# Decay differences of two chunks as two products a batch from sums spread over heads, and chunk 0's mixing placed behind its factors

## The chip, the core and the metric

The kernel runs on one core of a Trainium2 chip. Its engines run side by side, each through its own list of instructions in order: TensorE (PE: matrix products; PEld: the weight loads that go with them), VectorE (DVE), ScalarE (ACT), GpSimd (POOL), and SyncE (SP), which issues most DMA transfers. Products land in PSUM, in eight banks; everything else lies in SBUF, 128 partitions wide. The metric is the device time of one launch in microseconds.

## What is computed

A Mamba-2 state-space layer is followed by a feed-forward block with hardswish. Batch 4, 8 heads, 768 positions, head size 32, state size 16; the feed-forward has 256 inputs and 2048 hidden units. The reference, cut to what matters:

```python
log_a = np.log(np.clip(a, 1e-06, 1.0))
for c in range(nc):
    cum = np.cumsum(la, axis=-1)
    L = np.exp(cum[:, :, :, None] - cum[:, :, None, :]) * causal
    M = np.einsum('bhin,bhjn->bhij', Cc, Bc) * L
    y[:, :, sl] = np.einsum('bhij,bhjd->bhid', M, xc) + inter
    state = decay_full[:, :, None, None] * state + np.sum(Bx, axis=2)
...
h = x @ w_in
g = h * np.clip(h + 3.0, 0.0, 6.0) / 6.0
return g @ w_out
```

`x` of the last part is `y` with the heads laid side by side, 3072 rows of 256.

## The kernel before

The sequence is cut into 6 chunks of 128 positions, each handled as two halves of 64. For each chunk there is an attention part (decays, scores, mixing, state) and a feed-forward part (hidden layer, output layer). The program is one list written out by hand; each engine gets its instructions in that order, and tiles bring waits by themselves. The part of chunk 0 comes first; then the loop over `k` runs the feed-forward of chunk `k` and weaves the attention of chunk `k + 1` into it.

**Decays of chunks 0 and 1.** The running sum of log a (`cum`, L282) has 32 rows, one for each pair of batch and head. `in_three` (L286) splits the sums of the first 256 positions into three bf16 parts, 96 rows of `split`. For a batch, a PSUM bank `d` of 128 x 8 x 64 first takes the causal mask (L352). `diff_less` (L364) subtracts each position's own sum with one product of 512 columns. `diff_pick` (L373) adds the sum at the later position: `pick` has one column for each batch and head, with ones in that pair's three rows, so each head and half takes a product of its own, 64 columns wide, 16 a batch. `diff_exp` (L381) takes the exponential on ScalarE. `ends` (L412, GpSimd) scales B with the last column of the decays.

**Scores and mixing of chunk 0.** `turn_squares` (L481) transposes C on VectorE, `part_heads` (L488) parts its heads. `scores` runs the products L543 and those that go into the state (L555). `multiply` takes the sums out of PSUM on ScalarE (L571, L580) and multiplies the decays with the scores on VectorE (L585, four). `mix` has two parts `u`, four heads each: products L611 and then, for chunk 0, L516 from the middle state. `keep` copies the four quarters of y out of PSUM (L625, ScalarE) into `yT`. `renew` makes chunk 1's incoming state (L594, two L565 on VectorE). `turn_cum` transposes the later running sums on TensorE (L329), `by_token` negates them (L332). `busy` is a product with no use for the result (L506, one fp32 product in two passes).

**Weights.** They come as float64 in four quarters of `w_in` and four of `w_out`, 1 MB each, on the DMA queues, and `decode(i)` makes fp32 of them in five steps, one for each call of `weights(i, 1)`:

- step 1: L206 on ScalarE (copies the top 16 bits out); for quarter 0 also L209 and L213 on VectorE
- step 2: L223 and L225 on VectorE, which read what L206 wrote; then L209 for the others
- step 3: L229 on ScalarE
- step 4: L231 on ScalarE; L213 for the others; the load three quarters ahead (L143, SP)
- step 5: L236 and L249 on VectorE; L249 gives the finished weights

**Chunk 0's feed-forward.** `mlp_in` (L636) multiplies `yT` with the quarters of `w_in`, 16 blocks `f` of 512 columns in four rotating banks f0 to f3; ScalarE's L715 and VectorE's L720 make the hardswish of each, and steps of `decode` are woven between them. Then `first_out` (L735) multiplies with `w_out`. In that stretch VectorE also makes the split weights of the later chunks (L658, L663), the faded C of chunk 1 (L463) and its decays times scores (L585); L675 and L678 split its y, and the first product of the next hidden layer (L684) uses that.

**Banks.** Chunk 0's four `d` lie in f0 to f3, those of chunk 1 in the output banks (batches 0 and 1) and in y0 and y1 (batches 2 and 3). The scores take f0 to f3 again, the second halves of y take f0 and f1, `c_ps` of `turn_cum` takes f1, the bank of `busy` f0.

Of the kernel before, what the change touches and what calls it, by code (L numbers as in the profile page):

```python
# [21 lines left out]
def kernel(  # L22
# [172 lines left out]
    def decode(i):  # L195

        n = NK * FP * P  # L200
        top = raws[i].bitcast(U16).rearrange("p (n w) -> p n w", w=4)[:, :, 3]
        lo, hi = (raws[i].rearrange("p (n w) -> p n w", w=2)[:, :, w] for w in range(2))
        se = att.tile([P, 2, n], U16, name="wse")
        s, e = se[:, 0], se[:, 1]
        m = att.tile([P, n], U32, name="wm")
        nc.scalar.copy(out=s, in_=top)  # L206

        def significand():
            nc.vector.tensor_scalar(  # L209
                out=m, in0=hi, scalar1=0xFFFFF, scalar2=0x100000,  # L210
                op0=ALU.bitwise_and, op1=ALU.bitwise_or)
            yield
            nc.vector.scalar_tensor_tensor(  # L213
                out=m.bitcast(FP32), in0=lo, scalar=2.0 ** -32, in1=m, op0=ALU.mult,
                op1=ALU.add)
            yield

        parts_m = significand()
        if i == 0:
            next(parts_m)  # L220
            next(parts_m)
        yield
        nc.vector.tensor_scalar(  # L223
            out=e, in0=s, scalar1=0x7FF0, scalar2=None, op0=ALU.bitwise_and)
        nc.vector.tensor_scalar(  # L225
            out=s, in0=s, scalar1=0x8000, scalar2=None, op0=ALU.bitwise_and)
        next(parts_m, None)
        yield
        nc.scalar.activation(e.bitcast(BF16), e, AF.Relu, bias=bias_hi, scale=-8.0)  # L229
        yield  # L230
        nc.scalar.activation(e, e.bitcast(BF16), AF.Relu, bias=bias_lo, scale=-1.0)  # L231
        next(parts_m, None)
        if i and i + NRAW < 2 * NP:
            load_w(i + NRAW)
        yield
        nc.vector.tensor_tensor(out=e, in0=e, in1=s, op=ALU.bitwise_or)  # L236
        m, e = m.bitcast(FP32), e.bitcast(BF16)
        if i < NP:
            if i < 2:
                dst = att.tile([P, NK, FP * P], FP32, name="w32", tag="y", bufs=3)  # L240
            else:
                dst = ffn.tile([P, NK, FP * P], FP32, name="w32", tag=("wide", "back")[i - 2])
            first_in[i] = dst
            m, e = (t.rearrange("p (k f) -> p k f", k=NK) for t in (m, e))
        else:
            dst = w_out[:, (i - NP) * FP:(i - NP + 1) * FP, :]
            m, e = (t.rearrange("p (k f) -> p k f", k=FP) for t in (m, e))
        unit = 2.0 ** -20 if i >= NP else 2.0 ** -20 / Z
        nc.vector.scalar_tensor_tensor(  # L249
            out=dst, in0=m, scalar=unit, in1=e, op0=ALU.mult, op1=ALU.mult)  # L250
# [6 lines left out]
    picks = ffn.tile([P, G * N], BF16, name="picks", tag="u2")  # L257
    mid = pre[:G, 9].bitcast(BF16)[:, :2 * P]
    low = pre[:G, 10, :2 * P]

    cum = pre[:G, 4:6].rearrange("g t i -> g (t i)")[:, :S]
    cum_c = cum.rearrange("g (c p) -> g c p", p=P)
# [2 lines left out]
    def row_signs():  # L265
        with nc.allow_low_precision("zeros and ones"):
            nc.vector.tensor_reduce(
                out=pick, in_=ident[:, :pad].rearrange("g (r q) -> g q r", r=3), axis=AX.X,
                op=ALU.add)
        nc.scalar.mul(less, pick, -1.0)  # L270
        nc.gpsimd.tensor_copy(
            picks.rearrange("k (g n) -> k g n", n=N), pick.unsqueeze(2).to_broadcast([P, G, N]))
        nc.vector.tensor_reduce(
            out=parity, in_=head.rearrange("p q t -> p t q"), axis=AX.X, op=ALU.add)
# [11 lines left out]
    def in_three():  # L286
        first = cum[:, :2 * P]
        part = split.rearrange("g c p -> g (c p)")
        nc.vector.tensor_copy(part[:G], first)
        nc.vector.tensor_tensor(out=low, in0=first, in1=part[:G], op=ALU.subtract)  # L290
        nc.vector.tensor_copy(mid, low)
        nc.vector.tensor_copy(part[G:2 * G], mid)
        nc.vector.tensor_tensor(out=part[2 * G:pad], in0=low, in1=mid, op=ALU.subtract)
# [42 lines left out]
    def y_tile(name, dtype):  # L336
        return att.tile([P, NK, TB], dtype, name=name, tag="y", bufs=3)
# [28 lines left out]
            rhs=less[:, b * NH:(b + 1) * NH].unsqueeze(2).to_broadcast([P, NH, HT]),  # L366
            start=False, stop=True, skip_group_check=True)

    def diff_pick(c, b):
        for h in range(NH):  # L370
            for a, rows in enumerate(HALF):
                g = b * NH + h
                nc.tensor.matmul(  # L373
                    out=ds[c, b][rows, h], lhsT=pick[:, g:g + 1].to_broadcast([P, HT]),
                    rhs=split[:, c, rows], start=False, stop=True,
                    tile_position=(0, a * HT), skip_group_check=True)

    def diff_exp(c, b):
        if c not in Ls:
# [63 lines left out]
    def turn_b(c):  # L443

        t_ps = turn_ps(c, 1)
        transposes(c, 1, t_ps)
        nc.scalar.copy(out=turned(c)[0], in_=t_ps)
# [169 lines left out]
        if c and 1 in parts:  # L617
            from_state(c, 1)

    def keep(c):  # L620

        yTs[c] = y_tile("yT", FP32)
        for u in range(2):
            for a in range(2):
                nc.scalar.copy(out=y_half(yTs[c], a, u), in_=ys[c][a, u])  # L625

    def y_half(t, a, u):
        return t[:, u].rearrange("p (b i) -> p b i", b=NB)[:, :, HALF[a]]
# [330 lines left out]
    def weights(i, n):  # L959
        for _ in range(n):  # L960
            next(parts[i], None)


    def diff(c, *bs):
        for part in (diff_less, diff_pick):
            for b in bs:
                part(c, b)

    for c in range(2):
        for b in range(NB):  # L970
            diff_mask(c, b)
# [2 lines left out]
    row_signs()  # L974
    add_up(ends_at[0])
    in_three()
    for b in range(2):
        mask_again(0, b)
    diff(0, 0, 1)
    diff(0, 2, 3)  # L980
    weights(0, 1)
    for b in range(NB):
        diff_exp(0, b)
    first_eto()
    diff(1, 2, 3)
    weights(0, 1)
    for b in range(NB):
        ends(0, b)
    turn_b(0)
    diff(1, 0, 1)  # L990
    busy(1, ps.tile([P, NB * P], FP32, name="d", tag="f0"))
    weights(0, 1)
    diff_exp(1, 2)
    diff_exp(1, 3)
    turn_squares(bcs[0][0], turned(0)[2])
    part_heads(0)
    fade(0, HALF[1], nc.gpsimd)
# [4 lines left out]
    scores(0)  # L1002
    multiply(0)
    load_w(3)
    c_ps = ps.tile([P, NC, G], FP32, name="c_ps", tag="f1")
    turn_cum(c_ps)
    busy(1, ps.tile([P, NB * P], FP32, name="d", tag="f0"))
    weights(0, 1)
    weights(1, 1)
    by_token(c_ps)  # L1010
    mix(0)
    keep(0)
    weights(1, 3)
    renew(0)
    weights(1, 1)
    load_eto(1)
    load_bc(1)
    load_x(1)
# [7 lines left out]
    for k in range(NC):  # L1026
        gTs[k] = ffn.tile([P, NF, TB], FP32, name="gT")
        c, ahead = k + 1, k + 2
        if k == 0:
            for f in range(NF):  # L1030
                mlp_in(k, f)
                for i in weave.get(f, []):
                    weights(i, 1)
                if f in (6, 8):
                    diff_exp(c, f // 2 - 3)
            load_bc(ahead)
            weights(NP + 1, 1)
            weights(NP + 3, 1)
            weights(NP + 2, 3)
            sums = weight_sums()  # L1040
            for i in range(NP):
                for b in range(NB):
                    first_out(b, i, c)
                    if (i, b) == (0, 0):
                        weights(NP + 3, 1)
                        weights(NP + 2, 1)
                        weights(NP + 3, 3)
                        rows(ahead)
                    elif (i, b) == (1, 0):
                        for j in range(NP - 1):  # L1050
                            high_w(j)
                        for j in range(2):
                            low_w(j)
                            gap_w(j)
                    elif (i, b) == (2, 0):
                        turn(c, 1)
                        wake(c)
                        turn(c, 0)
                        low_w(2)
                        gap_w(2)  # L1060
                        high_w(NP - 1)
                        for p in range(2):
                            conceal(ahead, p)
                    elif (i, b) == (2, 3):
                        scores(c)
                        multiply(c)
                        renew(c)
                        decay_ends(ahead, 0)
                        decay_ends(ahead, 1)
                        next(sums)  # L1070
                    elif (i, b) == (3, 1):
                        results(c)
                        next(sums)
                        next(sums)
                        decay_ends(ahead, 2)
                        load_x(ahead)
            rows(ahead + 1)
            continue
# [89 lines left out]
```

## Time and profile before

| | us |
|---|---|
| median of 3 runs (lowest, highest) | 345.66 (345.23, 345.81) |
| the profiled execution's own time | 345.45 |
| its span, first to last instruction | 343.7 |
| TensorE busy, VectorE busy, ScalarE busy, GpSimd busy | 334.6, 220.1, 173.2, 142.7 |
| first L543 (scores of chunk 0) | 14.86 |
| first L636 (chunk 0's hidden layer) | 22.98 |
| first L735 (chunk 0's output layer) | 50.55 |
| first L684 (chunk 1's hidden layer) | 82.85 |

The granted clock is full in all 40 slices. A line of the timeline has start, duration, engine, source line, operation, tiles written and read, shapes, how many, and in brackets the idle time of the engine before it and what ended it. "issue" there means that no semaphore which the profile shows ended it. A row of a stage table has the stretch, its length, and for each engine the busy time and how many instructions. One L506, L543, L611 or L636 of the source is two passes on TensorE, and the profile counts passes. The queue q8 of the DMA view carries instructions.

### The profile page before, as it was taken

The numbers are of one execution on the slowest core, as the hardware profiler recorded it, in microseconds if no ns is written. First come the engines' busy times: TensorE is split into PE (matmuls) and PEld (weight loads), VectorE is DVE, ScalarE is ACT, GpSimd is POOL, SyncE is SP. The second block draws the span as 40 slices with busy tenths as digits, with TensorE's granted clock in tenths as the row PEclk, the third lists the DMA queues.
The fourth block names the chain that finished last, engine by engine and source line by source line (L and its number), as shares of the span: only waits on it lengthen the run. The fifth ranks groups of instructions, "written<-read, shape, count | busy, mean of one in ns | idle before, by whom it ended". The sixth has DMA issues, their size and how long they took to land.

```text
span 343.7 us, 8181 instructions
## 1 busy us (share of the span) xinstructions
PE 334.6 (97%) x3378; PEld 266.5 (78%) x3378; DVE 220.1 (64%) x357; ACT 173.2 (50%) x359; POOL 142.7 (42%) x139
## 2 busy tenths in 40 slices
PE   6889999999999999999999999999999999999996
PEld 2554448888778888888888888888887788888995
DVE  6689999999698647775438666447666324676011
ACT  4769878738874561564551564561564010565000
POOL 3300000093299923099611199610099400089500
PEclk9999999999999999999999999999999999999999
DMA  8888959206941057242029242051200010200010
GB/s 173 163 341 169 242 187 176 53 2 95 192 61 23 5 69 159 34 60 51 2 34 176 46 56 58 6 64 17 34 13 0 2 19 1 34 12 2 0 33 31
DMA packets 91605, 24.89 MB, mean 72 GB/s; under 512 B 84208, under 2 KB 87952, under 8 KB 91056
## 3 DMA queue, kind: packets, MB, share of 16 engines
q1 hardware_dynamic: 87184, 23.06, 34.8%
q10 hardware_dynamic: 4384, 1.31, 1.7%
q8 instruction: 26, 0.43, 0.5%
q14 instruction: 11, 0.09, 0.1%
HBM read 21.07 MB, written 3.29 MB: 71 GB/s over the span
## 4 chain that ended last, share of the span: by engine, by line
PE 75%; issue 11%; DMA 4%; DVE 2%; ACT 2%; POOL 2%; SPq 2%; POOLq 0%; DVEq 0%
PE h L684 31%; PE wb L861 13%; PE wc L861 8%; PE wa L861 8%; PE oa L794 4%; PE ob L794 4%; PE y L611 2%; PE y L516 2%; DMA raw<-in_moe_w_in_dram 2%; PE cb L543 2%; DMA eto<-cum_e 1%; ACT L L401 1%; POOL bs L412 1%; DMA pairs<-in_C_dram 1%; SPq L321 1%
## 5 line engine op out<-in xcount | busy, mean ns | idle before, releaser
L708 DVE SCALAR_TENSOR_TENSOR gT<-gT,h 128x512 f32<-128x512 f32 x80 | 54.9, 687 | 30.7 <-ACT gT L707 27.9
L707 ACT ACTIVATE gT<-h,half_up 128x512 f32<-128x512 f32 x80 | 55.1, 690 | 33.2 <-PE h L684 33.1
L780 POOL TENSOR_TENSOR s<-gT 128x512 f32<-128x512 f32 x20 | 25.8, 1288 | 66.4 <-DVE gT L708 66.4
L684 PE MATMUL h<-gap,w_gap 128*128 128x512 f32 x160 | 51.8, 409 | 0.0
L684 PE MATMUL h<-high,w_high 128*128 128x512 f32 x160 | 50.7, 398 | 0.1
L684 PE MATMUL h<-low,w_low 128*128 128x512 f32 x160 | 50.3, 395 | 0.0
L700 ACT ACTIVATE h<-h 128x512 f32<-128x512 f32 x40 | 23.5, 588 | 30.4 <-PE h L684 30.4
L684 PEld LDWEIGHTS h<-high,w_high 128*128 128x128 f32 x160 | 29.5, 188 | 8.5 <-DVE h L697 2.1
L684 PEld LDWEIGHTS h<-low,w_low 128*128 128x128 f32 x160 | 30.1, 188 | 7.2
L684 PEld LDWEIGHTS h<-gap,w_gap 128*128 128x128 f32 x160 | 29.9, 188 | 7.1 <-DVE gap L678 0.5
L401 ACT ACTIVATE L<-L,cum_n 128x64 f32<-128x64 f32 x128 | 31.6, 337 | 0.7 <-POOL L L162 0.7
L861 PE MATMUL wb<-s,w_out 128*128 128x256 f32 x128 | 30.7, 382 | 0.0
L419 POOL TENSOR_TENSOR tmp<-state,eto 128x256 f32<-128x256 f32 x5 | 3.6, 721 | 61.0 <-ACT eto L405 60.9
L735 PE MATMUL o<-w_out,gT 128*128 128x256 f32 x128 | 28.7, 381 | 0.0
L697 DVE TENSOR_SCALAR h<-h 128x512 f32<-128x512 f32 x40 | 27.7, 692 | 1.2 <-PE h L684 1.2
L636 PE MATMUL h<-yT,w 128*128 128x512 f32 x64 | 27.7, 594 | 0.0
L780 POOL TENSOR_TENSOR s<-s,gT 128x512 f32<-128x512 f32 x20 | 26.9, 1345 | 1.6
L585 DVE TENSOR_TENSOR L<-L,cb 128x512 f32<-128x512 f32 x24 | 15.3, 682 | 19.1 <-PE cb L543 16.3
L735 PEld LDWEIGHTS o<-w_out,gT 128*128 128x128 f32 x128 | 24.1, 190 | 3.8 <-issue 0.5
L861 PEld LDWEIGHTS wb<-s,w_out 128*128 128x128 f32 x128 | 24.0, 190 | 3.6
L412 POOL TENSOR_TENSOR bs<-B,L 128x128 f32<-128x128 f32 x24 | 13.7, 584 | 30.9 <-ACT L L401 25.8
L780 POOL TENSOR_TENSOR gT<-gT 128x512 f32<-128x512 f32 x20 | 25.9, 1294 | 0.0
(141 smaller groups left out, 534.3 us busy)
## 6 DMA issues: line engine op xcount, KB each, us to landing
raw<-in_moe_w_out_dram SPq DMA_DIRECT2D x4, 1024.0 KB
L<-cum_d SPq DMA_DIRECT2D x8, 512.0 KB
xt<-in_x_dram SPq DMA_DIRECT2D x6, 512.0 KB
raw<-in_moe_w_in_dram SPq DMA_DIRECT2D x3, 1024.0 KB
out_dram<-back SPq DMA_DIRECT2D x128, 16.0 KB
eto<-cum_e SPq DMA_DIRECT2D x20, 64.0 KB
B<-in_B_dram SPq DMA_DIRECT2D x5, 256.0 KB
raw<-in_moe_w_in_dram ACTq DMA_DIRECT2D x1, 1024.0 KB
```

The costliest lines, as they stand in the source:

```text
L401: nc.scalar.activation(Ls[c][:, b, h], Ls[c][:, b, h], AF.Exp, bias=cum_n[:, c, g:g + 1])
L412: nc.gpsimd.tensor_tensor(out=bss[c][:, hs], in0=Bs[c][:, hs], in1=Ls[c][:, b, :, HT - 1:HT].to_broadcast([P, NH, N]), op=ALU.mult)
L636: nc.tensor.matmul(out=h.rearrange("p r i -> p (r i)"), lhsT=first_in[f // FP][:, j, f % FP * P:(f % FP + 1) * P], rhs=yTs[k][:, j], start ...
L684: nc.tensor.matmul(out=h, lhsT=w[:, j, f * P:(f + 1) * P], rhs=y[:, j], start=(start and j == 0), stop=True, skip_group_check=True)
L697: nc.vector.tensor_scalar(out=h, in0=h, scalar1=-Z / UP, scalar2=None, op0=ALU.mult)
L700: nc.scalar.mul(h, h, -Z / UP)
L707: nc.scalar.activation(g, h, AF.Relu, bias=half_up, scale=UP * UP / 6.0)
L708: nc.vector.scalar_tensor_tensor(out=g, in0=g, scalar=UP, in1=h, op0=ALU.min, op1=ALU.mult)
L735: nc.tensor.matmul(out=o[:, b % 2], lhsT=gTs[0][:, f, b * P:(b + 1) * P], rhs=w_out[:, f], start=(f == 0 and b % 2 == 0), stop=True, skip_ ...
L780: nc.gpsimd.tensor_tensor(out=o, in0=p_, in1=q_, op=op)
L794: nc.tensor.matmul(out=bank[:, slot], lhsT=lhs[:, j], rhs=rhs[:, j], start=(clear and j == 0), stop=True, skip_group_check=True)
L861: nc.tensor.matmul(out=bank[:, slot], lhsT=lhs[:, j], rhs=rhs[:, j], start=(clear and j == 0), stop=True, skip_group_check=True)
```

## The change

The sixteen picking products of a batch become two. Two further sums of `pick` are made, `by_head` (ones in the three rows of each pair with that head, 8 columns) and `by_batch` (the same for batches, 4 columns). `spread_heads` multiplies a chunk's `split`, repeated over the heads, with `by_head`, repeated over the positions, on VectorE: 128 x 1024 in bf16. `diff_rows` then takes all heads of a half in one product of 512 columns, with `by_batch` as the other side.

The order changes too. All four `diff_less` of a chunk come ahead of its `diff_rows`; chunk 1's stand behind chunk 0's `ends`, its four `diff_rows` between two `busy` products, of which the second was behind `turn_cum` before. Chunk 0's mixing stands straight behind `multiply` and the last decoding step of quarter 0; its first half and its two copies come ahead of `turn_cum`, whose bank is now f2. Quarter 1's first decoding step, which has L209 and L213 in it now, moves behind the copies of y, `by_token` behind that. `renew(0)` moves into `first_out`.

```diff
         parts_m = significand()
-        if i == 0:
+        if i < 2:
             next(parts_m)
             next(parts_m)
...
+            for o, order in ((by_head, "k (b h) -> k h b"), (by_batch, "k (b h) -> k b h")):
+                nc.vector.tensor_reduce(
+                    out=o, in_=pick.rearrange(order, h=NH), axis=AX.X, op=ALU.add)
...
-    def diff_pick(c, b):
-        for h in range(NH):
-            for a, rows in enumerate(HALF):
-                g = b * NH + h
-                nc.tensor.matmul(
-                    out=ds[c, b][rows, h], lhsT=pick[:, g:g + 1].to_broadcast([P, HT]),
-                    rhs=split[:, c, rows], start=False, stop=True,
-                    tile_position=(0, a * HT), skip_group_check=True)
+    def spread_heads(c):
+
+        nc.vector.tensor_tensor(
+            out=spread[c], in0=split[:, c].unsqueeze(1).to_broadcast([P, NH, P]),
+            in1=by_head.unsqueeze(2).to_broadcast([P, NH, P]), op=ALU.mult)
+
+    def diff_rows(c, b):
+        for a, rows in enumerate(HALF):
+            nc.tensor.matmul(
+                out=ds[c, b][rows], lhsT=by_batch[:, b:b + 1].to_broadcast([P, HT]),
+                rhs=spread[c][:, :, rows], start=False, stop=True,
+                tile_position=(0, a * HT), skip_group_check=True)
...
-    def keep(c):
-
-        yTs[c] = y_tile("yT", FP32)
-        for u in range(2):
-            for a in range(2):
-                nc.scalar.copy(out=y_half(yTs[c], a, u), in_=ys[c][a, u])
+    def keep(c, u):
+
+        for a in range(2):
+            nc.scalar.copy(out=y_half(yTs[c], a, u), in_=ys[c][a, u])
...
     in_three()
+    spread_heads(0)
     for b in range(2):
         mask_again(0, b)
-    diff(0, 0, 1)
-    diff(0, 2, 3)
+    for part in (diff_less, diff_rows):
+        for b in range(NB):
+            part(0, b)
     weights(0, 1)
     for b in range(NB):
         diff_exp(0, b)
     first_eto()
-    diff(1, 2, 3)
     weights(0, 1)
     for b in range(NB):
         ends(0, b)
+    spread_heads(1)
+    for b in range(NB):
+        diff_less(1, b)
     turn_b(0)
-    diff(1, 0, 1)
     busy(1, ps.tile([P, NB * P], FP32, name="d", tag="f0"))
+    for b in (2, 3, 0, 1):
+        diff_rows(1, b)
     weights(0, 1)
     diff_exp(1, 2)
     diff_exp(1, 3)
+    busy(1, ps.tile([P, NB * P], FP32, name="d", tag="f0"))
     turn_squares(bcs[0][0], turned(0)[2])
...
     load_w(3)
-    c_ps = ps.tile([P, NC, G], FP32, name="c_ps", tag="f1")
+    weights(0, 1)
+    yTs[0] = y_tile("yT", FP32)
+    mix(0, (0,))
+    keep(0, 0)
+    c_ps = ps.tile([P, NC, G], FP32, name="c_ps", tag="f2")
     turn_cum(c_ps)
-    busy(1, ps.tile([P, NB * P], FP32, name="d", tag="f0"))
-    weights(0, 1)
+    mix(0, (1,))
+    keep(0, 1)
     weights(1, 1)
     by_token(c_ps)
-    mix(0)
-    keep(0)
-    weights(1, 3)
-    renew(0)
-    weights(1, 1)
+    weights(1, 4)
     load_eto(1)
...
                         weights(NP + 3, 3)
+                        renew(0)
                         rows(ahead)
```

## The prediction

> **What bounds the kernel now.** I read the page first, then the table by stage, then the timeline of each engine up to 90 us, the waits, and the DMA view in short stretches. All times below are of the one profiled execution, whose span is 343.7 us and whose own time is 345.45 us; the median of the runs is 345.66 us, 0.2 us more.
>
> The table by stage (columns: stretch, its length, then busy time and instructions of PE, PEld, DVE, ACT, POOL, then clock, DMA share, GB/s):
>
> ```profile
> 22.95:50.50 27.55, 27.55 (x68) 12.26 (x65) 24.97 (x39) 23.40 (x30) 0.00 (x0) 1.00 0.84 196
> 50.50:73.20 22.70, 22.70 (x171) 19.84 (x172) 22.32 (x27) 15.42 (x17) 5.28 (x5) 1.00 0.58 105
> ```
>
> From 22.95 us TensorE never rests, so one may think that the end moves with the start of the first feed-forward product (L636, 22.98). But VectorE is busy 22.32 of 22.70 us: the two run side by side. The waits of VectorE between 25 and 75 us are all of these:
>
> ```profile
> DVE wse L236 <- ACT wse L231: 1.4, 1, 1.4
> DVE L L585 <- PE cb L543: 0.8, 1, 0.8
> DVE gT L720 <- ACT gT L715: 0.6, 1, 0.6
> ```
>
> So VectorE's stream, which unpacks the weights, hangs on when its L236 at 25.73 may start. The timeline around it, TensorE first, then ScalarE and VectorE:
>
> ```profile
> 14.86 1.20 PE L543 MATMUL cb<-cT,bT 32*64 32x128 f32 x64 [0.94 <-DVE cT L488]
> ...
> 17.46 0.43 PE L329 MATMUL c_ps<-ident,pre 32*128 32x32 f32 x4 [0.61 <-DVE L L585]
> 17.81 1.12 PE L506 MATMUL d<-ident 128*128 128x512 f32 x2
> 18.87 0.94 PE L611 MATMUL y<-L,xt 64*32 64x64 f32 x60
> 20.74 0.30 PE L611 MATMUL y<-L,xt 64*32 64x64 f32 x4 [0.93 <-issue]
> ...
> 18.95 1.17 ACT L206 COPY wse<-raw 128x1024 uint16<-128x1024 uint16 x1 [1.16 <-DMA raw<-in_moe_w_in_dram]
> 23.10 0.37 ACT L625 COPY yT<-y 128x256 f32<-128x256 f32 x1 [0.26 <-PE y L516]
> 23.36 1.15 ACT L229 ACTIVATE wse<-wse,bias_hi 128x1024 bf16<-128x1024 uint16 x1
> ...
> 25.73 0.69 DVE L236 TENSOR_TENSOR wse<-wse 128x1024 uint16<-128x1024 uint16 x1 [1.43 <-ACT wse L231]
> 48.57 1.22 DVE L249 SCALAR_TENSOR_TENSOR w_out<-wm,wse 128x1024 f32<-128x1024 f32 x1
> 70.03 0.68 DVE L463 TENSOR_TENSOR csT<-t_ps,eto 128x512 f32<-128x512 f32 x1
> 73.97 1.28 DVE L585 TENSOR_TENSOR L<-L,cb 128x512 f32<-128x512 f32 x2 [0.77 <-PE cb L543]
> ```
>
> **The pause at 20.74.** The last four of the 64 L611 of one half wait 0.93 us for "issue", no semaphore. The queue of instructions explains it (packets, MB, share of 16 DMA engines; first of the span, then of 18.4 to 19):
>
> ```profile
> q8 instruction: 26, 0.43, 0.5%
> ...
> q8 instruction: 1, 0.02, 9.9%
> ```
>
> 26 packets are 16.5 KB each; 6756 TensorE instructions (3378 products, as many weight loads) over 26 are 260 each, 64 bytes apiece: blocks of 256. Up to the pause the stage table counts 10 + 146 + 128 + 66 = 350 products and as many loads: instruction 700. Boundaries then lie at 188, 444 and 700. Number 188 lies in the third group of L373, issued at about 10.5, and the DMA view has a packet between 10 and 11 us. Number 444 is the start of L555, at about 15.7, but no packet comes from 15.5 to 18.4, where queue 1 is full (93%, the second weight quarter); it comes in 18.4 to 19 (the second line above). After 700 at 20.74 the next comes in 24 to 24.5, when quarters three and four are in. I read: crossing one boundary orders the block after the next, and the order stands behind loads already issued. The block ordered at 15.7 was usable at 20.74. The Trainium skill ("Runtime: NRT & Kernel Launch", section "Instruction fetch mechanics") has blocks of 256 too, the next one fetched while the present one runs, and calls the crossing mostly hidden; by that the pause would not be the fetch, and the sum would be that of the first rival. The trace's 0.93 us without a semaphore decides for me.
>
> **The change part by part.**
>
> *Two reductions* before the running sum. Nearest rows: L273 (0.14 us, next start 0.07 later) and L267 (0.24, next 0.17 later): 0.07 to 0.17 each, together 0.24; `split` is ready at 7.74 in place of 7.50.
>
> *Spreads on VectorE, 128x1024 of 16 bits.* Not in the trace. Low end L236, two 16-bit inputs, 0.68; high end L249, 1.23. One operand repeats an element 128 times, unlike L236, so I take 1.22, with the next start after 1.14 (L213 at 8.26, L223 at 9.40). The skill ("Vector Engine (DVE) Microarchitecture Reference", 5.1) speaks against the change here: a repeated single element takes the packed rate away; by its rule 1.22, without it 0.68, a difference of up to 0.55 us at the scores and none where the pause decides.
>
> *Chunk 0's products.* L364 of 512 columns follow at 0.265 (two from 7.56 to 8.09). L373's 32 products of 64 columns took 0.63 (8.09 to 8.72), 20 ns each, where an eighth of 0.265 is 33, so the two halves overlap: 0.27 a batch (0.53 if not). Spread 7.78 to 9.00, first exponential at 9.55 in place of 8.57, the four done at 11.8 in place of 10.82. Behind them on ScalarE stand e's exponential, the copy of bT, L229, two exponentials and L231, which ends at 16.0; the next, L571, needs the scores' end (16.88 before). That hides it.
>
> *VectorE up to C's transpose.* L225 ends at 11.67 in place of 10.29, the second spread at 12.85; L481 starts at 12.8 in place of 12.63. *TensorE:* the first filler waits for e's exponential (12.23): 12.3 to 13.35; four batches 1.06; the second filler, moved here, 1.06 (17.81 to 18.87): the scores start at 15.45 in place of 14.86. Bounds: 15.05 by VectorE alone, 16.5 if the halves don't overlap.
>
> *Mixing.* L585 starts 1.26 after the scores, two take 1.2: the first half can start at 17.97. Then L611 0.79, L516 0.61, the transposes 0.35, again 0.79 and 0.61: the first product at 21.1, and its weights (L249, 20.45 before, 0.6 later) at 21.05. Against 22.98 this would be 1.85 early.
>
> *But the block boundary moves.* Over both chunks 128 products and as many loads become 16 and 16. Up to the scores there are now 92 instructions (312 before): masks 20, chunk 0 8 + 16, e 8, chunk 1's own sums 8, B's transposes 8, filler 4, chunk 1's rows 16, filler 4. 188 now falls 96 into the 128 of the scores (15.45 + 0.7 = 16.1, late by 0.4, still ahead of the next quarter's load, issued at 16.73 plus the scan's 0.2), and 444 falls 96 into the 128 of the first mixing half, at 18.6. Same order, same load ahead of it: usable at 20.74, a pause of 2.1 us. Then 0.2 + 0.61 + 0.35 + 0.79 + 0.61: the first product at 23.3, **0.3 later than before**.
>
> *ScalarE's order.* L206 of quarter 1 stood ahead of the copies of y (18.95); now it stands behind the last of them, and VectorE's L223 behind it. The last L625 starts 0.12 after the first product: 23.42. Then L206 23.68 to 24.8, L223 to 25.25, L229 at 25.3, L231 1.19 later, L236 1.18 later, at 27.67: **1.94 later than 25.73**. Queued behind L206 on ScalarE are L229, L231 and the first L715; on VectorE, behind L223, the whole stream. That L209 and L213 go ahead earlier helps nothing, they aren't what L236 waits for.
>
> *renew(0)* (L594 and two L565, 23.23 to 24.3, 1.07) was covered by the 1.43 us that VectorE waited for L231; now it stands at about 65 us, in the stretch with no gap: VectorE is 3.0 late from there. Who waits: L249 of w_out ended at 49.79, TensorE needs it at 50.55, slack 0.76: 1.2 late. L463 ended at 70.71, L516 ran at 72.24, slack 1.53: 1.5 late. At L585 0.77 of the 3.0 is taken up: 2.2; before the split of y (L675, 80.55) VectorE idled 0.55: 1.65. L678 ended at 83.42 and the next layer's L684 follows at once: **1.65 late**, and from there TensorE is full to 300 us, so it stays. 345.45 + 1.65 = 347.1; with the 0.2 to the median 347.3. On SP the fifth weight load needs quarter 1's buffer, so it follows L206, 24.8 in place of 23.39, and chunk 1's loads queue behind it; the fifth is unpacked from 40 us on, chunk 1's are used from 66 us on, so that costs nothing.
>
> **Rivals.**
>
> *The block comes in time* (no pause). The first product starts at 21.1, L206 at 21.5, L236 at 25.95, 0.2 late; with renew 1.3 at 65 us, less 0.77 and 0.55: nothing is left. 345.6, no change. For it: the fetch is inferred from counts.
>
> *Faster: the end follows the first product.* No pause, and VectorE's stream is not the bound: 1.85 early, 343.8. Deciding point: quarters unpacked more than 0.7 us earlier than now. Against it: VectorE's gaps after 26 us add up to 1.4 us.
>
> *The order falls behind the third quarter's load*, if the scores start after 16.2: it then waits for a second load, some 3 us more, 350.
>
> Chances: forecast 0.60, block in time 0.22, faster 0.10, behind the next load 0.08. The forecast's own bounds: the packet of 18.4 lasts 0.95 us (9.9% of 16 engines over 0.6), so the block could be usable at 19.45, first product 22.0, 346.0; 0.6 later than 20.74 gives 348. With the second case in, 345.2 to 348.2. A change under 0.2% (0.7 us) can't be told from none. Faster 0.11, same 0.22, slower 0.67.
>
> **What would show it.** TensorE standing still without a releaser inside the first half of L611, until about 20.7; an instruction packet at 18.4 to 19; L206 of quarter 1 behind the last copy of y; L236 near 27.7; L463 near 73.7. If the pause is gone and the first product starts by 21.3, the pause's reading is wrong; if L236 then also starts early and the end stays, VectorE's part is right.

## The result, and the profile after

The changed kernel takes 348.44 us (median of 7 runs, 346.86 to 348.99), the kernel before 345.48 us beside it (7 runs, 345.23 to 346.04): ratio 1.0075, 95% interval 1.0052 to 1.0099. It is slower, as forecast, by 3.0 us where 1.6 were forecast, and 0.2 us above the top of the range. The profiled execution took 348.88 us, span 347.2. (For two kernels of the experiments, e10 and e12, most runs lie over 1.5% above the fastest and are left out of the comparison; there, the median and the range of all runs stand.)

TensorE's timeline at chunk 0's mixing (start, duration, engine and line, instructions; in brackets the idle time before and what ended it). Line numbers are 6 to 10 higher than before: L553 is the scores, L621 the mixing's products, L526 its products from the middle state, L644 the first feed-forward product, L692 the next hidden layer's, L869 the later output layers'.

```profile
15.37 1.20 PE L553 MATMUL cb<-cT,bT 32*64 32x128 f32 x64
...
17.82 0.79 PE L621 MATMUL y<-L,xt 64*32 64x64 f32 x47 [0.46 <-ACT adds L581]
19.79 0.35 PE L621 MATMUL y<-L,xt 64*32 64x64 f32 x17 [1.18 <-issue]
...
22.43 1.98 PE L644 MATMUL h<-yT,w 128*128 128x512 f32 x4
```

The pause is where it was forecast, inside the first half of L621, but it ends at 19.79 and not at 20.74. The first product is 0.55 us earlier than before, not 0.3 later. The DMA view has the block's packet already between 17 and 18 us (first line: the whole span; second: this stretch):

```profile
q8 instruction: 25, 0.41, 0.5%
...
q8 instruction: 1, 0.02, 8.3%
```

ScalarE's and VectorE's timelines of the steps that the prediction followed, and TensorE's wait at the end of them:

```profile
22.82 1.12 ACT L206 COPY wse<-raw 128x1024 uint16<-128x1024 uint16 x1
24.43 1.15 ACT L229 ACTIVATE wse<-wse,bias_hi 128x1024 bf16<-128x1024 uint16 x1 [0.49 <-DVE wse L223]
...
23.97 0.43 DVE L223 TENSOR_SCALAR wse<-wse 128x1024 uint16<-128x1024 uint16 x1 [0.94 <-ACT wse L206]
26.80 0.69 DVE L236 TENSOR_TENSOR wse<-wse 128x1024 uint16<-128x1024 uint16 x1 [1.94 <-ACT wse L231]
49.63 1.22 DVE L249 SCALAR_TENSOR_TENSOR w_out<-wm,wse 128x1024 f32<-128x1024 f32 x1
66.11 0.42 DVE L604 TENSOR_TENSOR later<-mid,eto 128x256 f32<-128x256 f32 x1
72.28 0.68 DVE L473 TENSOR_TENSOR csT<-t_ps,eto 128x512 f32<-128x512 f32 x1
75.37 1.27 DVE L595 TENSOR_TENSOR L<-L,cb 128x512 f32<-128x512 f32 x2
82.42 0.76 DVE L683 TENSOR_TENSOR low<-y,high 128x256 fp32r<-128x256 f32 x2 [0.69 <-ACT high L680]
...
85.35 0.96 PE L692 MATMUL h<-gap,w_gap 128*128 128x512 f32 x3 [0.83 <-DVE gap L686]
```

L236 is 1.07 late (25.73 before), the faded C (L473) 2.25 (70.03), the decay's product L595 1.40 (73.97). After the wait at 85 us TensorE waits for none of it any more. But it stands still once more, at chunk 4, where before it did not. First the kernel before, then the changed one:

```profile
227.77 0.69 PE L516 MATMUL y<-csT,mid 32*64 32x64 f32 x32
228.40 1.99 PE L861 MATMUL wb<-s,w_out 128*128 128x256 f32 x8
```

```profile
227.03 1.49 PE L621 MATMUL y<-L,xt 64*32 64x64 f32 x128
228.44 0.68 PE L526 MATMUL y<-csT,mid 32*64 32x64 f32 x28
230.85 0.33 PE L526 MATMUL y<-csT,mid 32*64 32x64 f32 x4 [1.73 <-issue]
231.11 3.65 PE L869 MATMUL wb<-s,w_out 128*128 128x256 f32 x8
```

1.73 us for issue, no semaphore; then eight L869 take 3.65 us, where the same eight (L861) took 1.99 before. The table by stage (stretch, length, busy time and instructions of PE, PEld, DVE, ACT, POOL, granted clock, DMA share, GB/s) gives the reason for the second: a clock of 0.87 over these 13 us (third row), with 1.00 in the same stretch of before (fourth).

```profile
22.95:50.50 27.55, 27.19 (x64) 11.53 (x62) 23.52 (x36) 23.59 (x30) 0.00 (x0) 1.00 0.81 201
50.50:73.20 22.70, 22.52 (x117) 19.17 (x119) 22.29 (x31) 15.41 (x17) 4.75 (x5) 1.00 0.63 124
...
227.00:240.00 13.00, 11.27 (x194) 9.62 (x194) 4.66 (x9) 3.10 (x10) 1.48 (x2) 0.87 0.33 54
...
227.00:240.00 13.00, 13.00 (x173) 11.40 (x156) 8.69 (x17) 2.79 (x8) 1.04 (x2) 1.00 0.42 54
```

Where the time goes is seen best by one instruction followed through the span. The table below has the start of the same read of h by ScalarE, at eight places, minus its start in the profile of before (us; worked out from the traces; the columns e are experiments, told below; e10's profile is of its shortest run):

```
start before   after    e5     e4    e10     e9     e6
        84      1.87   1.09  -0.23  -0.30   1.98   3.43
       104      1.71   0.92  -0.41  -0.45   1.96   3.44
       136      1.68   0.87  -0.45  -0.48   1.96   3.44
       159      1.11   0.34  -1.01  -1.05   1.96   3.44
       208      0.67   0.42  -1.43  -1.49   1.95   3.44
       240      4.40   0.41   0.14  -1.49   2.65   3.45
       263      3.92  -0.06  -0.33  -1.97   2.65   3.44
       314      3.39  -0.57  -0.88  -2.50   2.67   3.47
```

For the changed kernel: 1.87 late when the second layer begins, 1.20 won back up to 208 us, 3.73 lost at the pause near 230 us (1.73 of pause, 1.66 of halved clock, the rest in the run-up), 1.01 won back after. Two terms that the prediction did not have, one of each sign, are larger than the one it had.

### The profile page after: what moved, and what is told of

Its sections match the earlier page's. It is cut to its first block, busy times and chain, and to the rows that moved or that the text cites. A ratio compares the mean times of both kernels' runs of the same rounds, so it can differ in the third digit from the quotient of the medians.

```text
span 347.2 us, 7965 instructions
## 1 busy us (share of the span) xinstructions
PE 334.5 (96%) x3266; PEld 266.3 (77%) x3266; DVE 223.7 (64%) x361; ACT 172.6 (50%) x359; POOL 144.8 (42%) x139
## 4 chain that ended last, share of the span: by engine, by line
PE 82%; DVE 5%; ACT 4%; DMA 3%; POOL 2%; issue 2%; SPq 1%; POOLq 0%; DVEq 0%
PE h L692 30%; PE wb L869 13%; PE wc L869 8%; PE wa L869 8%; PE o L743 5%; PE oa L802 4%; PE ob L802 4%; PE y L621 2%; PE h L644 2%; PE y L526 2%; DMA raw<-in_moe_w_in_dram 2%; PE cb L553 2%; ACT L L411 1%; POOL bs L422 1%; DVE gT L728 1%
## 5 line engine op out<-in xcount | busy, mean ns | idle before, releaser
L692 PE MATMUL h<-gap,w_gap 128*128 128x512 f32 x160 | 50.9, 403 | 0.9 <-DVE gap L686 0.8
L692 PE MATMUL h<-high,w_high 128*128 128x512 f32 x160 | 50.2, 395 | 0.2 <-DVE h L705 0.2
L692 PE MATMUL h<-low,w_low 128*128 128x512 f32 x160 | 49.3, 390 | 0.0
L692 PEld LDWEIGHTS h<-high,w_high 128*128 128x128 f32 x160 | 29.4, 188 | 8.1 <-DVE h L705 2.3
L692 PEld LDWEIGHTS h<-gap,w_gap 128*128 128x128 f32 x160 | 29.9, 188 | 7.4 <-DVE gap L686 1.1
L692 PEld LDWEIGHTS h<-low,w_low 128*128 128x128 f32 x160 | 30.0, 188 | 6.5
L869 PE MATMUL wb<-s,w_out 128*128 128x256 f32 x128 | 32.3, 398 | 0.0
L429 POOL TENSOR_TENSOR tmp<-state,eto 128x256 f32<-128x256 f32 x5 | 4.4, 881 | 62.6 <-ACT eto L415 62.5
L644 PE MATMUL h<-yT,w 128*128 128x512 f32 x64 | 28.2, 598 | 0.4 <-DVE w L249 0.4
L869 PEld LDWEIGHTS wb<-s,w_out 128*128 128x128 f32 x128 | 24.9, 197 | 4.0
L422 POOL TENSOR_TENSOR bs<-B,L 128x128 f32<-128x128 f32 x24 | 15.0, 636 | 30.6 <-ACT L L411 25.0
L595 DVE TENSOR_TENSOR L<-L,cb 128x512 f32<-128x512 f32 x24 | 15.3, 680 | 18.4 <-PE cb L553 15.7
L162 POOL TENSOR_SCALAR_AFFINE_SELECT L<-L 64x1024 f32<-64x1024 f32 (+1 forms) x16 | 19.9, 1250 | 14.6 <-DMA L<-cum_d 14.2
```

The source lines that it names most:

```text
L162: nc.gpsimd.affine_select(out=t[rows], in_=t[rows], pattern=pattern, compare_op=ALU.is_ge, fill=-1e5, base=base, channel_multiplier=-1)
L644: nc.tensor.matmul(out=h.rearrange("p r i -> p (r i)"), lhsT=first_in[f // FP][:, j, f % FP * P:(f % FP + 1) * P], rhs=yTs[k][:, j], start ...
L692: nc.tensor.matmul(out=h, lhsT=w[:, j, f * P:(f + 1) * P], rhs=y[:, j], start=(start and j == 0), stop=True, skip_group_check=True)
L869: nc.tensor.matmul(out=bank[:, slot], lhsT=lhs[:, j], rhs=rhs[:, j], start=(clear and j == 0), stop=True, skip_group_check=True)
```

## Experiments

Theory after the result: both pauses are waits for the next block of 256 instructions, and the change is slow because it has 224 TensorE instructions fewer ahead of them, so that the blocks end elsewhere. Rival: the order costs it (the copy L206 behind y, and `renew`).

**e1: the copy ahead of the mixing.**

```
-    mix(0, (1,))
-    keep(0, 1)
-    weights(1, 1)
...
     weights(0, 1)
+    weights(1, 1)
     yTs[0] = y_tile("yT", FP32)
     mix(0, (0,))
...
+    mix(0, (1,))
+    keep(0, 1)
     by_token(c_ps)
```

> The changed kernel with quarter 1's first decoding step put back ahead of the copies of y. Theory of ScalarE's order: L206 of quarter 1 runs at 18.3 (it stood at 22.82 in the changed kernel), L223 follows by_token at about 23.0 (23.97), VectorE's L236 starts at 25.8 (26.80), and the next hidden layer's first L692 that waited for the split of y comes about 0.8 us before 85.35. The first product stays at 22.4, the pauses without a releaser stay. Time: some 0.8 us under the changed kernel (347.6 where that has 348.4, 346.1 where no second pause falls). Rival, that GpSimd's chain from 68 us sets the next layer's start: it moves by less than 0.3 us.

347.92 us (6 runs, 346.68 to 350.34), ratio 1.0088 (1.0057 to 1.0120): by the times nothing gained. Lines of e1: the granted clock in 40 slices of 8.7 us (in tenths, 9 is 90% or more), then TensorE's, ScalarE's and VectorE's timelines:

```profile
PEclk9889999999999999999999999999999999999999
...
16.42 1.20 PE L553 MATMUL cb<-cT,bT 32*64 32x128 f32 x64
...
19.22 1.13 ACT L206 COPY wse<-raw 128x1024 uint16<-128x1024 uint16 x1
...
22.66 1.23 DVE L213 SCALAR_TENSOR_TENSOR wm<-raw,wm 128x1024 f32<-128x1024 uint32 x1
24.00 0.42 DVE L223 TENSOR_SCALAR wse<-wse 128x1024 uint16<-128x1024 uint16 x1
26.82 0.69 DVE L236 TENSOR_TENSOR wse<-wse 128x1024 uint16<-128x1024 uint16 x1 [1.94 <-ACT wse L231]
```

The copy starts 3.6 us earlier than in the changed kernel and L236 at the same time, but the two profiles can't be set side by side as they are: in e1's the clock is at half from 9.5 to 12.9 us, and its scores start at 16.42 in place of 15.37. Counted from the scores, L236 comes after 10.40 us in place of 11.43. That is the 1.0 us that was expected of L236 (25.8 against 26.80): the 0.94 us that L223 waited for the copy is gone, and L223 now stands straight behind L209, L213 and `by_token`. The gain doesn't show in the times. In this profile the clock was at half from 23.1 to 26.5 us too, and the second pause is there (1.62 us at 231.56).

**e2: `renew(0)` back** between `weights(1, 3)` and a last `weights(1, 1)` of quarter 1.

> The changed kernel with renew(0) put back between steps 4 and 5 of quarter 1. Theory of VectorE's stream: L236 of quarter 1 stays at 26.8, since VectorE waits 1.94 us there; from 66 us on the stream is 1.07 us earlier, L473 at 71.2 in place of 72.28, and the next hidden layer starts 0.7 to 1 us earlier. Rival, that GpSimd's chain sets it: under 0.3 us, since that chain starts from ScalarE's L415 at 67.73, which does not move.

347.43 us (12 runs, 345.58 to 349.11), ratio 1.0054 (1.0033 to 1.0075). The two intervals overlap, so by medians it isn't told from the changed kernel. Its two runs at a mean granted clock of 1.0 took 345.58 and 345.78 us, the changed kernel's one at 0.999 took 346.90: 1.1 to 1.3 us less, from three runs. In its profile TensorE does not wait at 85 us any more (0.83 us in the changed kernel), yet pauses for issue at 20.23 and 231.39 us. L236 is not at 26.8 as expected but at 28.22: TensorE's scores start 0.7 us later than in the changed kernel, and the clock is at half from 21.0 to 27.9 us.

**e4 and e6: one half of the change each.** e4 is the kernel before with the spread and two products a batch; e6 the kernel before, 16 products a batch, with the new order of mixing, copies and `renew`.

```
e4   +    spread_heads(0)
...
     -    diff(0, 0, 1)
     -    diff(0, 2, 3)
     +    for part in (diff_less, diff_rows):
     +        for b in range(NB):
     +            part(0, b)
e6   +    mix(0, (0,))
     +    keep(0, 0)
          turn_cum(c_ps)
     +    mix(0, (1,))
     +    keep(0, 1)
```

> The kernel before with the two products a batch and the spreads alone; mixing, copies, quarter 1 and renew in the order of before. Theory of blocks: 88 instructions up to the scores, block boundary 444 falls 88 into the 128 of the first mixing half, TensorE pauses there until about 19.8; first product at 22.1, L236 at 24.9, both 0.8 before the kernel before; the total of TensorE's instructions is that of the changed kernel, so the second pause near 230 us in the mixing of chunk 4 comes here too: 344.9 plus 1.7 to 3.4 where it falls, 346.6 to 348.3. Rival, that the products and the spreads themselves cost the time: first product and L236 later than before. Rival, that the second pause belongs to the moved steps: no pause near 230, time under 345.5.

> The kernel before with the changed order alone, the sixteen products a batch kept. Theory of blocks: boundary 700 falls just behind the first mixing half, pause until about 20.7, first product at 23.0, L206 behind the copies, L236 at 27.4 (25.73 before), renew in the full stretch; next hidden layer about 1.9 us later than before; all later boundaries stand where they stood, so no pause near 230 and a narrow spread of times: 347.2. Rival, that the order is harmless and the products cost the time: 345.5 or less.

e4: 344.54 us (11 runs, 344.12 to 346.50), ratio 0.9987 (0.9971 to 1.0004). e6: 348.92 us (5 runs, 348.39 to 350.34), ratio 1.0109 (1.0086 to 1.0132). Neither lies where the theory put it (346.6 to 348.3, and 347.2). Taken alone this says "the order costs it". The timelines of TensorE say more, first of e4, then of e6:

```profile
228.29 0.33 PE L526 MATMUL y<-csT,mid 32*64 32x64 f32 x3 [1.26 <-issue]
```

```profile
18.03 0.27 PE L516 MATMUL y<-csT,mid 32*64 32x64 f32 x1
20.25 1.12 PE L516 MATMUL y<-csT,mid 32*64 32x64 f32 x15 [1.95 <-issue]
```

e4 has the pause near 230 us without the new order, as expected, but not the one that was expected in chunk 0's mixing: that starts only at 19.54 there, 2.4 us after the block's packet (17.10). e6, with the old number of instructions, doesn't have the one near 230 us. In e6 the mixing has been moved ahead to where its block is 1.95 us away, and the clock is at half from 20.0 to 26.8 us behind it: that, and the wait of 0.83 us at 87 us that `renew` leaves, is in the 3.43 us of its column, and nothing is added after 84 us.

**e5, e7, e8: the same code, its blocks moved.** 38 small products (152 instructions) go where TensorE waits for the decay; their output is overwritten by `mask_again`. e5 is the changed kernel with them, e7 is e4 with them, e8 the changed kernel with them and with both moves of e1 and e2.

```
+    def fill(n):
+        for j in range(n):
+            rows, d0 = HALF[j % 2], 32 * (j // 2 % 4)
+            nc.tensor.matmul(
+                out=ds[0, j % 2][d0:d0 + 32, 0], lhsT=ident[rows, :32], rhs=ident[rows, :HT],
+                start=True, stop=True, tile_position=(j % 2 * HT, d0), skip_group_check=True)
...
     spread_heads(0)
+    fill(38)
     for b in range(2):
         mask_again(0, b)
```

> The changed kernel with 38 small fp32 products (152 instructions) ahead of the masks of chunk 0, where TensorE waits for the decay anyway; their result is overwritten, so nothing that is computed changes. They move every boundary between instruction blocks 152 instructions ahead. Theory (the pauses at 19.8 us and at 230.9 us are waits for instruction blocks, and the halved clock behind the second is their result): neither pause is there, no half-speed window lies after 20 us, and the time falls from 348.4 to about 345.9 us (345.4 to 346.6). What is left over before (345.3) is then the price of the order itself. Rival (the loss is the order: the quarter-1 weights and the decay difference come late): 347.6 to 348.5 us, pauses gone or not.

> The two products a batch in the order of before, with the same 38 small products ahead of the masks. Without them this kernel took 344.54 us and its trace has a pause of 1.26 us at 228.3 us. Theory (blocks): that pause is gone, and the time is 343.3 to 344.2 us, below before (345.3) by more than 0.3%. Rival (the pause at 228 us is made up later, because VectorE ends the second half anyway): 344.4 to 344.7 us.

> The changed kernel with the copy of quarter 1's top part ahead of chunk 0's mixing and renew back between the first quarters' steps, and with the 38 small products. Theory (pauses and halved clock cost about 2.5 us, the late quarter-1 weights and renew the other 0.5 to 0.8): 344.6 to 345.6 us, the fastest kernel with chunk 0's mixing straight behind its factors, no pause above 0.5 us between 19 and 24 us or near 230 us. Rival (the order itself costs 2 us or more): 346.5 us or above.

e5: 344.91 us (11 runs, 344.68 to 347.55), ratio 0.9982 (0.9962 to 1.0002). e7: 344.42 us (5 runs, 343.92 to 344.68), 0.9965 (0.9953 to 0.9977). e8: 344.91 us (8 runs, 344.33 to 345.40), 0.9980 (0.9970 to 0.9991). TensorE in e5, at the two places:

```profile
17.77 0.94 PE L629 MATMUL y<-L,xt 64*32 64x64 f32 x64 [0.46 <-ACT adds L589]
21.31 1.98 PE L652 MATMUL h<-yT,w 128*128 128x512 f32 x4
...
228.20 0.69 PE L534 MATMUL y<-csT,mid 32*64 32x64 f32 x32
228.82 1.99 PE L877 MATMUL wb<-s,w_out 128*128 128x256 f32 x8
```

152 more instructions make the changed kernel 3.5 us shorter (3.2 by the two ratios): both pauses gone (one of 0.39 us is left, at 168.7), eight of the output layer's products in 1.99 us again. The theory holds and the rival falls as the main cause. The time is below what the theory gave (345.4 to 346.6); the table's column shows why, an unforeseen gain, most of it after 136 us. e8 equals e5: its profile has a new pause of 1.68 us at 75.8 us, which can have eaten what the two moves bring. e7 and e8 beat before with intervals clear of 1. e7 is the fastest here by its median, though it pauses 1.45 us at 75.5 us and misses the 343.3 to 344.2 that was expected.

**e9: the kernel before with 12 of the small products**, nothing of the change.

> The kernel before, nothing of the change in it, with 12 of the small products (48 instructions) ahead of the masks. Its block boundaries then lie in the mixing of chunk 4 about where they lie in the changed kernel (some 54 and 310 instructions into a stretch of 320, instead of 102 and past its end). Theory (two boundaries in one fast stretch make TensorE wait for the second block): a pause of 1.2 to 1.8 us appears near 228 us where before has none, in some runs with a half-speed window behind it; 345.8 to 347.2 us. Rival (the pause at 230.9 us comes from the changed order, not from where the boundaries lie): no pause there, 345.2 to 345.6 us.

348.41 us (6 runs, 347.95 to 350.09), ratio 1.0092 (1.0074 to 1.0111): 48 instructions whose result is thrown away, executed in idle time, cost the kernel before as much as the whole change did. TensorE's timeline, then the stretch behind the pause:

```profile
18.61 0.67 PE L619 MATMUL y<-L,xt 64*32 64x64 f32 x36
20.94 0.45 PE L619 MATMUL y<-L,xt 64*32 64x64 f32 x28 [1.67 <-issue]
...
230.68 0.44 PE L524 MATMUL y<-csT,mid 32*64 32x64 f32 x11 [0.39 <-issue]
```

```profile
23.10:26.60 3.50, 3.50 (x15) 1.72 (x11) 1.35 (x4) 2.64 (x4) 0.00 (x0) 0.51 0.76 286
```

The time is above the 345.8 to 347.2 expected, and the place of the loss was expected wrongly: 2.0 us of it are lost early (the block arrives at the same time as before, but is needed 24 products sooner, and the clock is at half for 3.4 us behind it) and only 0.7 us near 230 us, where 1.2 to 1.8 were expected.

**e10 to e13: 104 instructions (136 in e12)**, chosen by counting so that no two block ends fall into one chunk's mixing. e10 is e4, e11 the changed kernel, e12 the kernel before, e13 the changed kernel with both moves.

> The two products a batch in the order of before, with 26 small products (104 instructions) ahead of the masks in place of 38 (152) or none. With none its trace paused at 228.3 us, with 38 at 75.5 us (1.45 us). Counting 256 instructions a block on from the pauses seen so far, 104 more instructions put no two boundaries into one stretch of chunk mixing. Theory (blocks): no pause of 0.3 us or more that nothing but issue explains, anywhere after 24 us, and 343.2 to 344.1 us, the fastest of all. Rival (a pause at 75 us is made up within the next 20 us and only the one near 230 us costs): as with 38, 344.3 to 344.6 us.

> The changed kernel with 26 small products (104 instructions) ahead of the masks. Theory (blocks): no pause for issue after 24 us, near 230 us none, 344.3 to 345.2 us, as with 38 products (344.91) or up to 0.5 us faster. Rival (152 instructions were special, for instance because the longer filler kept TensorE busy): 346 us or above.

> The kernel before, nothing of the change in it, with 34 small products (136 instructions) ahead of the masks: by the same count no pause for a block after 24 us, and its one pause of 0.93 us at 20.7 us moved or gone. This gives the change a ground without pauses to be compared on. Theory (where the blocks end is worth some tenths here, and 48 instructions cost 2.8 us only by their place): 344.4 to 345.5 us, against 348.41 us with 12 products. Rival (any filler slows the kernel before): 347 us or above.

> The changed kernel with the copy of quarter 1's top part ahead of chunk 0's mixing and renew back between the first quarters' steps, with 26 small products. With 38 it took 344.91 us and paused 1.68 us at 75.8 us. Theory: that pause is gone, 343.8 to 344.7 us; the difference to the changed kernel with 26 products, nothing else altered, is what the two moved steps cost (0.3 to 0.8 us). Rival (the two moved steps cost nothing once no block is late): equal to that kernel within 0.2 us.

```
e10  349.38 us, 12 runs, 342.98 to 350.21
e11  346.88 us, 12 runs, 344.47 to 348.84, ratio 1.0037 (1.0011 to 1.0063)
e12  351.54 us,  6 runs, 344.40 to 353.05
e13  345.81 us, 12 runs, 343.25 to 347.48, ratio 0.9998 (0.9970 to 1.0025)
```

As medians these are misses; only the shortest runs lie where they were expected, or up to 0.6 us below. After 26 us the count came true: no pause for issue of 0.3 us in any of the four (e12 has 0.28 at 86.9 us). But a block now ends inside chunk 0's mixing while two more megabytes of weights are being loaded, and its fetch can fall behind them. TensorE in e13, the stretch after the pause, and the DMA view from 20.8 to 21.4 us:

```profile
19.88 0.64 PE L629 MATMUL y<-L,xt 64*32 64x64 f32 x39
23.15 0.66 PE L629 MATMUL y<-L,xt 64*32 64x64 f32 x25 [2.63 <-issue]
```

```profile
22.90:29.70 6.80, 6.55 (x47) 3.53 (x48) 4.20 (x10) 4.04 (x6) 0.00 (x0) 0.50 1.05 316
```

```profile
q1 hardware_dynamic: 59, 0.24, 97.7%
q8 instruction: 1, 0.02, 9.8%
```

In e13 the block end before the pause is crossed at 17.28, the two loads are issued from 17.29, and the packet starts at 20.95; in the profile of e11, with the same count of instructions, the crossing and the loads come at 17.14, the packet starts at 18.14, and there is no pause. e12's profile has two such pauses (2.63 and 2.50 us) and the clock at half for 6.8 us. That the long runs of e10 and e11 are runs in which the fetch lost this race fits their granted clocks (0.985 to 0.995, against 1.0 in the shortest), but none of them was profiled: it is argued, not shown.

## Why the prediction was right and where it was not

**Up to the scores** it held: `split` done at 7.74 (7.74 forecast), first exponential 9.50 (9.55), eight row products in 1.05 us (1.06), scores 15.37 (15.45). The first spread took 1.23 us (1.22), the second 1.43, beside four GpSimd products that took 2.79 us in place of 1.53. With that the trace agrees with the Trainium skill ("Vector Engine (DVE) Microarchitecture Reference", 5.1), which speaks against the packed rate for a repeated element.

**The moved block end** was the right mechanism, with one wrong term: "Same order, same load ahead of it: usable at 20.74". The boundary was crossed at 16.05, the packet started at 17.10, not at 18.5 as before, and TensorE went on at 19.79, 0.95 us sooner. So L236 was 1.07 late in place of 1.94.

**The copy behind y** is most of that 1.07: VectorE has done L209, L213 and L338 at 23.03, and waits 0.94 us more for the copy until L223 at 23.97; with the copy ahead (e1) L236 came 1.0 us earlier, counted from the scores. The forecast had this step at its place, and too late by about as much as the pause was too long (L236 0.87, the pause's end 0.95). "That L209 and L213 go ahead earlier helps nothing" leaves out that they bound the gain: without the pause the two come out level. In e5 the copy runs from 21.69 and L223 starts at 22.90, in e8 the copy is at 18.16 and L223 at 22.94.

**`renew`** took 1.0 us at 66.1, as priced, and its path to 85 us was 1.88 late at L692 (1.65 forecast), though by another way: L595 was only 1.4 late, and the split of y (L683), which waited 0.69 for ScalarE's L680, was 1.87 late again where 0.55 was to be made up. That `renew` is behind it rests on the wait there: 0.83 in the changed kernel, e6 and e11, 0.70 in e1, 0.33 in e5, none over 0.25 in e2, e8 and e13, where it is moved back. So the 1.65 came nearly true by luck, by errors of opposite sign: a smaller delay of L236, and less made up behind it.

**"From there TensorE is full to 300 us, so it stays"** is the step that failed. It missed the second pause and its halved clock (3.7 us), although the prediction had itself found the blocks and did not carry their count on to the later chunks: chunk 4's mixing is a stretch of 320 instructions in 2.1 us, in which two block ends now lie. And it missed a gain of 2.2 us (1.20 + 1.01 in the table). The groups of L692, of e6 (old products, L682) and of the changed kernel, busy time and mean of one:

```profile
L682 PE MATMUL h<-gap,w_gap 128*128 128x512 f32 x160 | 51.7, 408 | 0.8 <-DVE gap L676 0.8
L682 PE MATMUL h<-high,w_high 128*128 128x512 f32 x160 | 50.7, 398 | 0.1
L682 PE MATMUL h<-low,w_low 128*128 128x512 f32 x160 | 50.3, 395 | 0.0
```

```profile
L692 PE MATMUL h<-gap,w_gap 128*128 128x512 f32 x160 | 50.9, 403 | 0.9 <-DVE gap L686 0.8
L692 PE MATMUL h<-high,w_high 128*128 128x512 f32 x160 | 50.2, 395 | 0.2 <-DVE h L705 0.2
L692 PE MATMUL h<-low,w_low 128*128 128x512 f32 x160 | 49.3, 390 | 0.0
```

From start to start these products are mostly 236 or 231 ns apart in before and e6, 227 or 226 in the changed kernel and e10. Every kernel with the two products a batch and the spreads has it, whatever its order or filler, none without them does. What in them does it is open; it wasn't tried. `by_head` and `by_batch` are two small tiles put into the first pool, so what is allotted after them may lie elsewhere in memory; that this is the cause is a guess.

**The rival "block comes in time"** (345.6 us) was nearly built in e5: no early pause, first product at 21.31 (21.1). At 84 us it is still 1.09 late where the rival had nothing left; it ends at 344.91 only by the gain in the products. Where neither kernel pauses, the order alone costs 1.5 us at 84 us (e11 is 1.21 late there, e10 0.30 early), and the shortest runs of e13 (five of 343.25 to 343.67) against those of e11 (344.47 and 344.65) say that the two moves are about 1 us of it. By L236, at 25.71 in e5 and 25.76 in e8, the copy's place costs nothing where there is no pause, so this would be `renew`; the shortest runs of e13 were not profiled.

## What to carry to other kernels

An edit that removes or adds instructions moves every block end behind it; count instructions in blocks of 256 and see which ends fall into stretches of many short instructions, and what is being loaded when they are crossed, before giving a change of 1% to its order or its arithmetic. A neutral filler in idle time is a cheap test of this, and a comparison of two kernels at one alignment can mislead: the change measured +0.75%, with 152 idle instructions in front no loss (-0.18%, 0.9962 to 1.0002), with 104 +0.37%. The four kernels with a block end in chunk 0's mixing while large loads are queued (e10 to e13) spread most in time, 4.2 to 8.7 us (e10: best run 342.98, median 349.38 us); that the fetch is what spreads them is argued, not shown.

## What the runs showed of the hardware that was not expected

**Block fetches.** Counting TensorE's own register and wait instructions too, every pause for issue of 0.39 us or more behind 10 us, in all fourteen traces, falls on an instruction number 193 + 256 n or the next one, and ends 2.2 to 2.8 us after the start of an instruction packet. The table has most of them (worked out from the traces):

```
kernel   number   packet at   TensorE goes on   later by
before      705       18.50             20.74       2.24
after       449       17.10             19.79       2.69
after      4801      228.24            230.85       2.61
e1         4801      228.94            231.56       2.62
e4         4801      225.87            228.29       2.42
e6          705       17.99             20.25       2.26
e7         1473       73.03             75.46       2.43
e8         1473       73.02             75.77       2.75
e9          705       18.57             20.94       2.37
e12         961       23.31             25.83       2.52
e13         705       20.95             23.15       2.20
```

In the five pauses of the table behind 70 us the packet starts 0.7 to 1.1 us after the block end before is crossed (227.22 to 228.24 in the changed kernel), and TensorE goes on 3.1 to 3.7 us after that crossing (2.2 in e9 at 230.68). So, as an estimate from these five, a block of 256 instructions that is gone through in less time leaves TensorE without instructions; the 320 of chunk 4's mixing take 2.1 us. Around 20 us, beside the weight loads, the packet came later: 1.05 us after the crossing in the changed kernel, 2.50 before, 3.67 in e13. The Trainium skill ("Runtime: NRT & Kernel Launch", "Instruction fetch mechanics") has the blocks of 256 and the fetch of the next one during the present one, and calls the crossing mostly hidden. Here most of the some 25 crossings of a trace show no pause; those that do cost 0.4 to 2.6 us.

**The clock after a pause.** After some pauses the granted clock is 0.5 for 3.41 us or twice that: 231.3 to 234.7 in the changed kernel, 23.2 to 26.6 in e9, 22.9 to 29.7 in e13. After others (19.79 in the changed kernel, 75.46 in e7) it stays at 1.0. In e1 and e4 a stretch at half comes from 9.5 and 9.3 us, with no pause for issue ahead of it. One such stretch in full work costs up to 1.7 us, and as it comes in some runs and not in others it spreads them: the changed kernel's seven runs have mean clocks from 0.984 to 0.999, e7's five all 1.0. What decides it is open: by the traces TensorE was busy for 0.30 to 0.72 of the 3.41 us ahead of a halved stretch, and for 0.48 to 0.78 ahead of others that were not halved.
